# A quarter of batch 4's first product by Strassen's scheme, with four changes of order: the first chain, the w2 loads, S4, batch 5's attention

## The chip, the cores and the metric

The kernel runs on one core of one Trainium2 chip. The metric is the device time of one execution in microseconds. The core has a matrix engine (TensorE, PE in the profile), three engines for the rest (VectorE = DVE, ScalarE = ACT, GpSimd = POOL) and a queue engine (SyncE = SP) that here only issues DMA transfers. Each engine takes its instructions strictly in the order of the program and waits for the others by semaphores.

## What is computed

For each of 8 batches: linear attention with a cosine feature map over 8 heads (576 positions, head size 64), then a mixer: a low-rank product over the positions (U 576x32, V 32x576) with a residual, and a two-layer product over the 512 channels with 2048 hidden units.

```python
r = np.maximum(x, 0.0)                       # phi, for q and k
phi = np.concatenate([r * cos_w, r * sin_w], axis=-1)
kv = einsum('bhsf,bhsd->bhfd', k_p, v);  z = k_p.sum(axis=2)
x = einsum('bhsf,bhfd->bhsd', q_p, kv) / (einsum('bhsf,bhf->bhs', q_p, z) + 1e-6)
# heads side by side: x is [8, 576, 512]
u = x + (x.transpose(0, 2, 1) @ U @ V).transpose(0, 2, 1)
out = u + np.maximum(u @ w_ch1, 0.0) @ w_ch2
```

The large products are u @ w_ch1 (the first product) and the one with w_ch2 (the second).

## The kernel before

The 576 positions of a batch are 512 that are worked on as four chunks c of 128, and a tail of 64; the tails of two batches (a pair) are put together to one chunk of 128. All matmul operands are bf16, sums are float32 in PSUM (eight banks, which the code names by tags: "g" with three buffers, "T", "X" of two banks, "oA", "oB" or "O").

**The line of units.** After batch 0's attention everything is one hand-laid list of units of TensorE work (`slots`), most of them 0.9 us long. For each pair: the first product of the even batch (16 units of one hidden block j each), its second product, the first product of the odd batch, four units of the pair's tail, the second product of the odd batch, and for the first two pairs four more for the tail's second product. `starts[b]` is the slot at which batch b's first product begins. A second list (`todo`, by slot) holds what is issued behind each unit: the attention of the next batch, the feature maps, the DMA transposes and the loads. So the order on every engine follows from the slot numbers that `attention_plan` (L1097) gives.

**First product.** A plain unit is `g1_main` (L676): four matmuls of 512 columns into a "g" bank, then one ScalarE pass with the ReLU. `MIXED` (L789) names batches in which quarters m = 0 and 2 of the 16 hidden blocks go by Strassen's scheme instead: `g1_part` (L602) makes seven products of four matmuls of 256 columns each, and the eight units of HALF (L1015) interleave them with the four plain blocks of the next quarter. Parts 1, 6, 5, 3 add up in one bank (al_ps, tag T) that ScalarE copies out between them (pw), parts 2, 7, 4 in others (be_ps); VectorE adds and rectifies. They read differences of blocks of w1 (sa, made once, L571) and of u transposed (tb, `uT_form`, L590, four VectorE operations in the four slots ahead of `starts[b]`). Before, batches 3 and 5 are mixed in both quarters, batch 7 wholly, the others plain.

**Second product.** From batch 1 on it goes by Strassen's scheme: `w_part(b, n)` (L843) for n = 0 to 13 is half of one of seven steps, eight matmuls of 256 columns. I call n a half step. Step s is half steps 2s and 2s + 1. Steps 1, 2 and 3 open a bank each, steps 0 and 4 share one, step 5 adds into the bank of step 2, and step 6 into that of step 3, after VectorE has read it. Steps 1, 2, 3 and 5 read sums of hidden blocks (`hid_form`, L814): S1, S2 = S1 - hid, S3, S4 = hid - S2, each made in two halves on VectorE; the first halves beside the first product (L1035), the second halves by the table in L867. At half step 3 VectorE makes w_sum, then one block of the output on VectorE and two on GpSimd (L886 to L891).

**Attention of the next batch.** `kv_pair`, five `x_unit`s (matmuls, then denominator, reciprocal and product on VectorE), `A_unit` (U), `u_va` (V), `u_add` on VectorE, then `utr_dma`: the transposes of u (uT) as DMA transposes from SP's queue. The plan places them at slots counted from G = `starts[b - 1]`. For an odd batch b the tail follows (`u_tail`, and uT_tl). The loads of batch b + 1 and the transposes of q (q_tlT, q_pT) also go through SP's queue, in slot order.

**Batch 0** has no batch to hide behind. `first_chain` (L1232) runs its attention by hand: features, transposes of q, denominators (`den_mm`), kv in two groups of four heads, x, and uT on TensorE: `open_mm` puts x transposed into a bank, and `uTd_mm` adds the low-rank term (32 rows of the array each, d-th row group) and so closes it. `w1_load` and `w2_load` (L100, L106) are loads of 512 KB that GpSimd issues; a small copy into `mark` makes GpSimd wait for an event first (L1311, L1317, L1326). `gate` (L1340) does the same on SP: batch 2's loads wait for w2's second chunk.

Of the kernel before, what the change touches and what calls it, by code (L numbers as in the profile page):

```python
# [10 lines left out]
FP32 = mybir.dt.float32  # L11
BF16 = mybir.dt.bfloat16
# [5 lines left out]
def kernel(  # L18
# [93 lines left out]
    def cast(eng, o, i):  # L112
        if eng is nc.scalar:
            nc.scalar.activation(out=o, in_=i, func=AF.Copy, bias=0.0, scale=1.0)  # L114
        else:
            eng.tensor_copy(out=o, in_=i)  # L116
# [216 lines left out]
    def kv_unit(b, hg, tag, bufs, eng=None):  # L333
        if b not in kv_sb:
            kv_sb[b] = pool.tile([P, H, E], BF16, tag="kv", bufs=2, name="kv")
        n = D if b == 0 else E
        acc = bank([P, 4, n], FP32, tag, bufs, "kv_ps")
        for i in range(4):
            h = hg * 4 + i
            for c in range(5):  # L340
                nc.tensor.matmul(
                    out=acc[:, i, :],
                    lhsT=k_p[b][:, c, h, :] if c < 4 else k_tl[:, h, :],
                    rhs=v0[:, h, c, :] if b == 0 else vx_of(b, c, h),
                    start=(c == 0),
                    stop=(c == 4),
                )
        cast(eng or V_, kv_sb[b][:, hg * 4 : hg * 4 + 4, 0:n], acc)

    def kv_pair(b, tag, bufs):  # L350
        kv_sb[b] = pool.tile([P, H, E], BF16, tag="kv", bufs=2, name="kv")
# [200 lines left out]
    def uTd_evac(b, d, eng):  # L552
        cast(eng, uT[b][:, d, :, :], uT_ps[b, d])
# [232 lines left out]
                in_=o_s[i * TS : i * TS + TS, :],  # L786
            )

    MIXED = {3: (0, 2), 5: (0, 2)}  # L789
    HD = DM // 2  # L790
    KB = NJ // 2
    w2_h = w2_bf.rearrange("p (k i) n -> p k i n", i=2)
# [50 lines left out]
    def w_part(b, n):  # L843
# [16 lines left out]
        for k_ in range(half * 4, half * 4 + 4):  # L860
            for g in range(2):
# [2 lines left out]
                    start=(opens and k_ == 0 and g == 0),  # L864
                    stop=(k_ == KB - 1 and g == 1), skip_group_check=not opens,
                )
        for f in ({0: (4,), 2: (3,)} if b == B - 1 else {0: (1, 2), 2: (3,), 4: (4,)}).get(n, ()):  # L867
            hid_form(b, f, 1)
        if half == 0:
            return  # L870
# [219 lines left out]

    ODDX = (5, 8, 11, 13, 15)
    QORD = (4, 0, 1, 2, 3)

    def feature(b, f, c, i, eng):
        f(b, c, (eng, None) if i == 0 else (None, eng))

    def attention_plan(b):  # L1097
# [3 lines left out]
        def put(at, f, *a):  # L1101
            plan.append((at, lambda: f(b, *a)))
# [17 lines left out]
        else:  # L1120
# [16 lines left out]
            kv_at = X0  # L1137
            if late:
                kv_at, x_at = G + 3, [G + i for i in (5, 8, 13, 16, 18)]
            elif b - 1 in MIXED:  # L1140
                kv_at, x_at = G + 1, [G + i for i in ODDX]
            a_at = x_at[4] + (3 if b in (4, 6) else 2)
            u_at = a_at + 1
            a_bank = T1 if b == 3 else OB
# [6 lines left out]
            put(x_at[n], x_unit, c, *((O1, X1)[n % 2] if b < 4 else X1))  # L1151
        put(a_at, A_unit, *a_bank, A_)
        put(u_at, u_va, (0, *X1), (2, *O1) if b < 4 else (2, OA, OB))
        d0 = 2 if odd and b - 1 in MIXED else 0
        put(u_at, u_add, d0)
        put(u_at + 2, u_add, 2 - d0)
        put(u_at + 2, utr_dma, d0, d0 + 2)
        put(u_at + 4, utr_dma, 2 - d0, 4 - d0)
        if odd:
            put(*((u_at + 1, u_tail, *T1) if b < 4 else (u_at + 3 + d0, u_tail, *X1S)))  # L1160
            put(u_at + 4 + d0, utr_dma, 4, 5)
        if b < B - 1:
            for at_, t in zip(at_load, loads(b + 1)):
                plan.append((at_, t))
# [50 lines left out]
    def open_mm(b, d, t, cs):  # L1215
        for c in cs:
            nc.tensor.matmul(
                out=t[:, c, :], lhsT=x_bf[b][:, c, d * P : d * P + P], rhs=ident,
                start=(c == 0), stop=False,
            )  # L1220
# [11 lines left out]
    def first_chain(b, xz, z, v_ps):  # L1232
# [6 lines left out]

        d = xz[:, 1, 0:480].rearrange("p (c h n) -> p c h n", h=H, n=12)  # L1240
        rec = pool.tile([P, 5, H], FP32, tag="rec5", bufs=1, name="rec5")
        for h in (0, 2):
            cast(V_, v0[:, h : h + 2], vst[:, h : h + 2])
        cast(V_, z_sb, z[:, :, 0])
        qtr_evac(b, 2, V_, t_q[2])
        cast(V_, v0[:, 4:H], vst[:, 4:H])
        qtr_evac(b, 4, A_, t_q[4])
        kv_unit(b, 0, *G3, A_)
        cast(A_, V_bf, v_ps.rearrange("r (c p) -> r c p", c=4))
        den_mm(b, d, (0, 1, 3, 2, 4))  # L1250
        recip(rec, d[:, :, :, 0])
        x0 = [xh_mm(b, c, 0, *G3) for c in ORD[0:2]]
        kv_unit(b, 1, *T1, A_)
# [10 lines left out]
        cast(A_, A_of(b)[0:TS, :], a_ps[0:TS, :])  # L1264
        for i, (tag, bufs) in enumerate((OA, OB, T1)):
            uT_ps[b, i] = bank([P, 4, P], FP32, tag, bufs, "uT_ps")
        open_mm(b, 0, uT_ps[b, 0], range(4))
        x1.append(xh_mm(b, ORD[4], 4, *G3))
        for n in range(2, 5):
            xh_norm(b, ORD[n], 4, rec, x1[n])  # L1270
        uTd_mm(b, 0)
        uTd_evac(b, 0, A_)
        open_mm(b, 1, uT_ps[b, 1], range(4))
        uTd_mm(b, 1)
        uTd_evac(b, 1, A_)
# [17 lines left out]
    for c in TL:  # L1293
        q_prep(0, c, FEATS[c])
        qtr_mm(0, c, 0, H, t_q[c])
        keep_warm(1, "X", 1)
    for c, eng in zip(TL[0:2], (V_, A_)):
        qtr_evac(0, c, eng, t_q[c])
    xz = ps.tile([P, 2, 512], FP32, tag="X", bufs=1, name="xz")
    z = xz[:, 0, 0:384].rearrange("p (h n) -> p h n", n=48)  # L1300
# [22 lines left out]
    for h0 in (0, 4):  # L1323
        load_odd(vst, v, 1, h0, h0 + 4)
        load_even(vst, v, 1, h0, h0 + 4)
    G_.tensor_copy(out=mark, in_=kst[0:TS, 3, 4, 0:1])  # L1326
    for n in range(4):
        w2_load(n)
    g1_open(0, (0, 0), (0, 1))
    uTd_close(0, 2, V_)  # L1330
    uTd_close(0, 3, A_)
    g1_open(0, (0, 2), (1, 0), (1, 1), (1, 2))
    q_prep(1, 4, (V_, A_))
    q_prep(1, 0, (V_, V_))


    def at(j, *thunks):
        beside.setdefault(j, []).extend(thunks)

    def gate(src):  # L1340
        nc.sync.dma_start(out=mark2, in_=src)
# [102 lines left out]
```

## Time and profile before

| | us |
|---|---|
| median of three runs (292.41 to 292.49) | 292.44 |
| the profiled execution | 292.46 |
| its span | 290.7 |

| engine | busy us | share of the span | instructions |
|---|---|---|---|
| TensorE | 285.7 | 98% | 3062 |
| VectorE | 224.5 | 77% | 447 |
| ScalarE | 162.2 | 56% | 282 |
| GpSimd | 67.5 | 23% | 104 |

The granted clock of TensorE is 1.00 in every stretch but the last (0.99). A row of the timeline has the start, the length, the engine, the line of the kernel, the operation, what is written and read, the shape and the count; in square brackets stands the idle time before it, and who ended it. Matmuls overlap: a row's length contains the way through the array, so costs are taken from start to start, or from the chain of waits, whose pieces do not overlap. A group row has a count, then the busy time, then the mean length in ns, then the idle time ahead of it.

### The profile page before, as it was taken

Reading aid. Unit: us, or ns where it says so; the run is one execution under the profiler, and the core shown is the slowest. Engines: PE = TensorE matmul, PEld = TensorE weight load, DVE = VectorE, ACT = ScalarE, POOL = GpSimd, SP = SyncE. Lnnn points to the kernel's source line nnn. Section 1 sums busy time; section 2 is a strip of 40 time slices with the busy share of each in tenths; the row PEclk is TensorE's granted clock in tenths of the full one; section 3 lists DMA queues with packets and bytes.
Section 4 is the critical chain, followed back from the end, with each engine's and each line's share of the span. In section 5 each row is a group of like instructions: output and inputs, shape, how many; then the busy total and the mean of one; then the engine's idle time right before and its main releaser. Section 6 shows DMA issues by size and latency. Waiting matters only on the chain.

```text
span 290.7 us, 7417 instructions
## 1 busy us (share of the span) xinstructions
PE 285.7 (98%) x3062; PEld 206.0 (71%) x3062; DVE 224.5 (77%) x447; ACT 162.2 (56%) x282; POOL 67.5 (23%) x104
## 2 busy tenths in 40 slices
PE   8999999999999999999999999999999999999995
PEld 6876455545987546876986646876888548999884
DVE  4879748887898778948896377848899687769974
ACT  2965651576593456966693456966791562067100
POOL 8340500050052303640042500441031102100210
PEclk9999999999999999999999999999999999999999
DMA  6999999999939999799838995999186304120023
GB/s 200 337 283 253 261 186 264 297 245 221 287 86 153 231 357 194 216 278 265 237 58 181 229 281 100 249 249 291 18 145 77 148 12 81 49 99 0 2 87 132
DMA packets 85447, 53.32 MB, mean 183 GB/s; under 512 B 53990, under 2 KB 83078, under 8 KB 85414
## 3 DMA queue, kind: packets, MB, share of 16 engines
q1 hardware_dynamic: 78998, 41.62, 60.5%
q0 software_dynamic: 6272, 11.17, 15.8%
q8 instruction: 24, 0.39, 0.6%
q14 instruction: 9, 0.07, 0.1%
q10 hardware_dynamic: 144, 0.07, 0.1%
HBM read 36.86 MB, written 9.44 MB: 159 GB/s over the span
## 4 chain that ended last, share of the span: by engine, by line
PE 96%; DVE 2%; issue 1%; DVEq 0%
PE g_ps L684 29%; PE w_ps L862 28%; PE gt_ps L715 5%; PE o_ps L755 5%; PE al_ps L635 5%; PE be_ps L635 4%; PE w_ps L202 3%; PE x_ps L431 3%; PE kv_ps L356 2%; PE ot_ps L775 2%; PE ot_ps L963 2%; PE a_ps L457 1%; PE va_ps L487 1%; DVE u_bf L498 1%; PE t_ps L374 1%; PE t_ps L386 1%
## 5 line engine op out<-in xcount | busy, mean ns | idle before, releaser
L684 PE MATMUL g_ps<-uT,w_bf 128*128 128x512 bf16 x378 | 91.2, 379 | 0.0
L691 ACT ACTIVATE hid<-g_ps 128x512 bf16<-128x512 f32 x96 | 57.0, 597 | 44.6 <-PE g_ps L684 37.6
L684 PEld LDWEIGHTS <-w_bf 128*128 128x128 bf16 x378 | 34.3, 98 | 33.5
L874 POOL TENSOR_TENSOR o_sb<-w_sum,u_bf 128x512 f32<-128x512 f32 x14 | 22.1, 1595 | 117.5 <-DVE w_sum L874 117.5
L862 PEld LDWEIGHTS <-hid 128*128 128x128 bf16 x448 | 43.6, 98 | 5.6
L862 PEld LDWEIGHTS <-S 128*128 128x128 bf16 x336 | 32.3, 98 | 4.9 <-issue 0.5
L862 PE MATMUL w_ps<-T,hid 128*128 128x256 bf16 x224 | 26.9, 273 | 0.0
L862 PE MATMUL w_ps<-w_bf,hid 128*128 128x256 bf16 x224 | 26.9, 273 | 0.0
L862 PE MATMUL w_ps<-T,S 128*128 128x256 bf16 x224 | 26.3, 273 | 0.0
L652 DVE TENSOR_TENSOR hid<-pw,be_ps 128x512 bf16<-128x512 f32 x24 | 16.4, 685 | 11.9 <-ACT pw L114 7.6
L114 ACT ACTIVATE pw<-al_ps 128x512 f32<-128x512 f32 x24 | 14.2, 597 | 18.2 <-PE al_ps L635 17.4
L874 DVE TENSOR_TENSOR o_sb<-o_sb,w_ps 128x512 f32<-128x512 f32 x28 | 19.1, 682 | 4.9 <-PE w_ps L862 4.3
L498 DVE TENSOR_TENSOR u_bf<-x_bf,va_ps 128x1024 bf16<-128x1024 bf16 (+1 forms) x20 | 19.5, 1001 | 4.0 <-PE va_ps L487 3.9
L441 DVE TENSOR_TENSOR x_bf<-x_ps,rec 128x512 bf16<-128x512 f32 x28 | 19.3, 691 | 1.0
L305 ACT ACTIVATE k_p<-kst,sinw 128x512 bf16<-128x512 f32 x26 | 17.7, 712 | 0.0
L729 POOL DMA_DIRECT2D out_dram<-o_sb x12 | 7.6, 632 | 41.2 <-DVE o_sb L763 20.9
L116 POOL CAST v_ext<-vst 128x512 bf16<-128x512 f32 x24 | 15.6, 694 | 6.1 <-issue 3.7
L715 PE MATMUL gt_ps<-uT_tl,w_bf 128*128 128x128 bf16 x256 | 16.4, 219 | 0.0
L755 PE MATMUL o_ps<-w_bf,hid 128*128 128x512 bf16 x64 | 15.6, 379 | 0.0
L830 DVE TENSOR_TENSOR S<-hid,S 128x1024 bf16<-128x1024 bf16 x14 | 15.4, 1097 | 0.1
L715 PEld LDWEIGHTS <-w_bf 128*128 128x128 bf16 x256 | 15.0, 98 | 0.4
L305 ACT ACTIVATE q_p<-qst,cosw 128x512 bf16<-128x512 f32 x21 | 14.4, 712 | 0.0
(188 smaller groups left out, 472.7 us busy)
## 6 DMA issues: line engine op xcount, KB each, us to landing
qst<-in_q_dram SPq DMA_DIRECT2D x14, 512.0 KB, 6.3
kst<-in_k_dram SPq DMA_DIRECT2D x14, 512.0 KB, 8.2
vst<-in_v_dram SPq DMA_DIRECT2D x12, 512.0 KB, 7.9
out_dram<-o_sb POOLq DMA_DIRECT2D x12, 512.0 KB, 5.2
w_bf<-in_moe_w_ch_dram POOLq DMA_DIRECT2D x8, 512.0 KB, 10.2
out_dram<-o_sb SPq DMA_DIRECT2D x4, 512.0 KB, 3.0
qst<-in_q_dram SPq DMA_DIRECT2D x2, 640.0 KB, 5.8
kst<-in_k_dram SPq DMA_DIRECT2D x2, 640.0 KB, 13.8
```

Of the source, the lines that this page charges most:

```text
L116: eng.tensor_copy(out=o, in_=i)
L305: nc.scalar.activation(out=o, in_=i, func=AF.Relu, bias=0.0, scale=w)
L441: nc.vector.tensor_tensor(out=x_of(b, c, rows).rearrange("p (g i d) -> p g i d", g=2, d=D), in0=view[:, :, :, 0:D], in1=rec[rows].unsqueez ...
L498: nc.vector.tensor_tensor(out=u_bf[b][:, d0 : d0 + n], in0=x_bf[b].rearrange("p c (d n) -> p d c n", n=P)[:, d0 : d0 + n], in1=t.rearrange ...
L635: nc.tensor.matmul(out=res[:, k_, :], lhsT=lhs[:, d, k_, :], rhs=rhs[:, d, :], start=(opens and k_ == 0 and d == 0), stop=(k_ == 1 and d = ...
L652: V_.tensor_tensor(out=o, in0=x, in1=res, op=ALU.add)
L684: nc.tensor.matmul(out=g_ps.rearrange("p (c t) -> p c t", c=4), lhsT=w1_bf[:, d, j * P : j * P + P], rhs=uT[b][:, d, :, :], start=(d == 0) ...
L691: nc.scalar.activation(out=hid[b][:, j, :], in_=g_ps, func=AF.Relu, bias=0.0, scale=1.0)
L715: nc.tensor.matmul(out=g_ps[:, jj, :], lhsT=w1_bf[:, d, j * P : j * P + P], rhs=uT_tl[pr][:, d, :], start=(d == 0), stop=(d == 3),)
L755: nc.tensor.matmul(out=o, lhsT=hid[0][:, j, cc * P : cc * P + P], rhs=w2_bf[:, j, :], start=(j == 0), stop=(j == NJ - 1),)
L862: nc.tensor.matmul(out=res[:, g, :], lhsT=lhs[:, k_, g * P : g * P + P], rhs=rhs[:, k_, :], start=(opens and k_ == 0 and g == 0), stop=(k_ ...
L874: eng.tensor_tensor(out=o, in0=x, in1=y, op=ALU.add)
```

## The change

1. Batch 4's quarter m = 0 becomes mixed; the list of batches with both quarters mixed gets a name (`FULL`). Two rules that asked "is batch b - 1 mixed" now ask for `FULL`. What follows for batch 4 is that its first eight units are those of HALF, that `uT_form` runs ahead of it, and that the first halves of its S forms go to units 9, 11, 17 and 18 of its own (8 to 11 before); the last two lie in its second product.
2. For batch 5, whose attention runs beside batch 4, kv moves from slot G - 2 to G + 1, the x units from G + 0, 2, 4, 6, 8 to G + 5, 8, 11, 13, 15, `A_unit` to G + 17, `u_va` to G + 18; uT's transposes to G + 20 and G + 22, and the tail one slot later than the formula had it. Batch 4's second product begins at G + 16. On SP's queue batch 7's loads of v now stand ahead of batch 5's uT, and batch 6's q_tlT between the two of them.
3. In the second product, the second half of S4 is made at half step 1 instead of 4 (batches 1 to 6).
4. In batch 0's chain the third copy of q transposed comes ahead of k's features on VectorE; kv of the first four heads and the denominators alternate; uT is opened for d = 0 and 1, then closed for both, then copied out; d = 2 and 3 are closed ahead of the six openings of the first product, which stood around them.
5. GpSimd waits for batch 1's last q transposed, in slot 6, instead of for batch 1's k, before it issues the four w2 loads.

```diff
-    MIXED = {3: (0, 2), 5: (0, 2)}
+    MIXED = {3: (0, 2), 4: (0,), 5: (0, 2)}
+    FULL = [b for b, ms in MIXED.items() if 2 in ms]
...
-        for f in ({0: (4,), 2: (3,)} if b == B - 1 else {0: (1, 2), 2: (3,), 4: (4,)}).get(n, ()):
+        for f in ({0: (4,), 2: (3,)} if b == B - 1 else {0: (1, 2), 1: (4,), 2: (3,)}).get(n, ()):
             hid_form(b, f, 1)
...
+    X5 = (5, 8, 11, 13, 15)
...
+            elif b - 1 in FULL:
+                kv_at, x_at = G + 1, [G + i for i in ODDX]
             elif b - 1 in MIXED:
-                kv_at, x_at = G + 1, [G + i for i in ODDX]
+                kv_at, x_at = G + 1, [G + i for i in X5]
...
-        d0 = 2 if odd and b - 1 in MIXED else 0
+        d0 = 2 if odd and b - 1 in FULL else 0
...
         if odd:
-            put(*((u_at + 1, u_tail, *T1) if b < 4 else (u_at + 3 + d0, u_tail, *X1S)))
-            put(u_at + 4 + d0, utr_dma, 4, 5)
+            late_t = 1 if b - 1 in MIXED and b - 1 not in FULL else 0
+            put(*((u_at + 1, u_tail, *T1) if b < 4 else (u_at + 3 + d0 + late_t, u_tail, *X1S)))
+            put(u_at + 4 + d0 + late_t, utr_dma, 4, 5)
...
-        for h in (0, 2):
-            cast(V_, v0[:, h : h + 2], vst[:, h : h + 2])
+        cast(V_, v0[:, 0:2], vst[:, 0:2])
         cast(V_, z_sb, z[:, :, 0])
-        qtr_evac(b, 2, V_, t_q[2])
+        cast(V_, v0[:, 2:4], vst[:, 2:4])
         cast(V_, v0[:, 4:H], vst[:, 4:H])
         qtr_evac(b, 4, A_, t_q[4])
-        kv_unit(b, 0, *G3, A_)
+        kv_sb[b] = pool.tile([P, H, E], BF16, tag="kv", bufs=2, name="kv")
+        acc = bank([P, 4, D], FP32, *G3, "kv_ps")
+        kv0_mm(b, acc, (0, 1))
+        den_mm(b, d, (0, 1, 2))
+        kv0_mm(b, acc, (2, 3))
         cast(A_, V_bf, v_ps.rearrange("r (c p) -> r c p", c=4))
-        den_mm(b, d, (0, 1, 3, 2, 4))
+        cast(A_, kv_sb[b][:, 0:4, 0:D], acc)
+        den_mm(b, d, (3, 4))
...
-        open_mm(b, 0, uT_ps[b, 0], range(4))
+        for i in range(2):
+            open_mm(b, i, uT_ps[b, i], range(4))
         x1.append(xh_mm(b, ORD[4], 4, *G3))
...
-        uTd_mm(b, 0)
-        uTd_evac(b, 0, A_)
-        open_mm(b, 1, uT_ps[b, 1], range(4))
-        uTd_mm(b, 1)
-        uTd_evac(b, 1, A_)
+        for i in range(2):
+            uTd_mm(b, i)
+        for i in range(2):
+            uTd_evac(b, i, A_)
...
-    for c, eng in zip(TL[0:2], (V_, A_)):
+    for c, eng in zip(TL[0:3], (V_, A_, V_)):
         qtr_evac(0, c, eng, t_q[c])
...
-    G_.tensor_copy(out=mark, in_=kst[0:TS, 3, 4, 0:1])
-    for n in range(4):
-        w2_load(n)
-    g1_open(0, (0, 0), (0, 1))
-    uTd_close(0, 2, V_)
-    uTd_close(0, 3, A_)
-    g1_open(0, (0, 2), (1, 0), (1, 1), (1, 2))
+    for d in (2, 3):
+        uTd_mm(0, d)
+    uTd_evac(0, 2, V_)
+    uTd_evac(0, 3, A_)
+    g1_open(0, *((d, j) for d in range(2) for j in range(3)))
...
+    def w2_all():
+        G_.tensor_copy(out=mark[0:1], in_=q_pT[1][0:1, 3, 0, 0:1])
+        for n in range(4):
+            w2_load(n)
+
+    at(6, w2_all)
```

`kv0_mm` is new: the five matmuls over the chunks of `kv_unit` for the heads that it is given, without the copy.

More of the change, by code (lines that the diff above doesn't have):

```diff
@@ L348, in kv_unit, with kv0_mm @@
         cast(eng or V_, kv_sb[b][:, hg * 4 : hg * 4 + 4, 0:n], acc)
+    def kv0_mm(b, acc, hs):
+        for h in hs:
+            for c in range(5):
+                nc.tensor.matmul(
+                    out=acc[:, h, :], lhsT=k_p[b][:, c, h, :] if c < 4 else k_tl[:, h, :],
+                    rhs=v0[:, h, c, :], start=(c == 0), stop=(c == 4),
+                )
     def kv_pair(b, tag, bufs):
```

## The prediction

> **What bounds the kernel now.** I read the page first, then the chain of waits in order of time, then the timelines of TensorE, VectorE and GpSimd around each edit.
>
> ```profile
> span 290.7 us, 7417 instructions
> ...
> PE 96%; DVE 2%; issue 1%; DVEq 0%
> ```
>
> The span is 290.7 us, the profiled execution itself took 292.46 us, so 1.76 us lie around the span; the three plain runs have a median of 292.44 us, and I treat the two as one number. The second row is the chain that ended last: 96% of it is TensorE. So the time is the sum of what TensorE executes plus the few places where it stands still. Anything on another engine counts only where TensorE waits for it. Following TensorE's starts through the timeline, I find waits in batch 0's chain (16 to 19 us) and two more:
>
> ```profile
> 151.65 1.91 PE L862 MATMUL w_ps<-w_bf,hid 128*128 128x256 bf16 x16
> 153.73 1.91 PE L862 MATMUL w_ps<-w_bf,S 128*128 128x256 bf16 x16 [0.17 <-DVE o_sb L874]
> ...
> 217.63 1.91 PE L862 MATMUL w_ps<-w_bf,hid 128*128 128x256 bf16 x16
> 219.56 1.91 PE L862 MATMUL w_ps<-w_bf,S 128*128 128x256 bf16 x16
> ```
>
> These are starts, lengths and counts. Sixteen such matmuls take 1.75 us from start to start (16 x 0.109, below); here 153.73 - 151.65 = 2.08 and 219.56 - 217.63 = 1.93. So TensorE loses 0.33 us in batch 3's second product and 0.18 us in batch 5's, both ahead of step 5 (half step 10), which adds into the PSUM bank that VectorE must first have read in step 2.
>
> **The quarter of batch 4.** It replaces 16 plain matmuls of 512 columns by 7 parts of 4 matmuls of 256 columns.
>
> ```profile
> 101.16 2.59 PE g_ps L684 x12
> ...
> 258.00 1.31 PE al_ps L635 x12
> ```
>
> From the chain: 2.59 / 12 = 0.216 us and 1.31 / 12 = 0.109 us. 16 x 0.216 = 3.45 us go, 28 x 0.109 = 3.06 us come: **-0.40 us**. Beside TensorE, ScalarE keeps four passes, and VectorE gets three additions (0.69 each) with three rectifications (0.3) and four differences of uT (0.4): 4.6 us.
>
> ```profile
> 160.00:180.00 20.00, 20.00 (x207) 10.95 (x204) 12.34 (x26) 10.93 (x19) 3.92 (x7) 1.00 0.91 213
> ```
>
> In this view of stretches the columns are TensorE, its weight loads, VectorE, ScalarE, GpSimd, the granted clock, DMA. VectorE works 12.34 of the 20 us around batch 4's first product, so 7.7 us hide the 4.6, and ScalarE is no fuller; batches 3 and 5 run the same eight units today with no TensorE wait in them. Cost: nothing. Without that cover a late addition would hold a PSUM bank, and TensorE for as long.
>
> The Trainium skill speaks against this edit (TensorE: Matmul & The Clock Gate, Back-to-back issue gap): in a sustained stream a matmul of 512 columns costs 131 ns and one of 128 columns 81 ns, so narrow ones are dear. By an estimate between those figures, about 98 ns for 256 columns, the quarter would lose 0.6 us instead. The trace disagrees with both figures (216 and 109 ns); the sum goes by the rows.
>
> **Batch 5's attention moves later.** With batch 4 mixed, kv and the x units of batch 5 slide to units 1, 5, 8, 11, 13, 15, and its A, va and u_tail groups leave batch 4's first product for its second. TensorE does the same work, with the same number of changes between 32-row and 128-row matmuls. But VectorE now has three additions to u (and u_tail), and two half forms (S4, S3), in the second product, behind which the step 2 read waits. I work out that queue, counted from the first matmul W of the second product.
>
> ```profile
> 171.27 0.16 DVE L421 TENSOR_SCALAR rec<-x_ps 128x8 f32<-128x8 f32 x1
> ...
> 172.30 0.68 DVE L830 TENSOR_TENSOR S<-S,hid 128x1024 bf16<-128x1024 bf16 x1
> ...
> 179.21 0.69 DVE L830 TENSOR_TENSOR S<-hid 128x1024 bf16<-128x1024 bf16 x1 [0.90 <-ACT hid L691]
> 179.94 0.69 DVE L830 TENSOR_TENSOR S<-S,hid 128x1024 bf16<-128x1024 bf16 x1
> 180.55 0.47 DVE L307 TENSOR_SCALAR q_tl<-qst,sinw 64x512 bf16<-64x512 f32 x1
> 180.94 0.47 DVE L307 TENSOR_SCALAR q_p<-qst,sinw 128x512 bf16<-128x512 f32 x1
> ```
>
> The last x unit ends at W, its three VectorE instructions take 172.30 - 171.27 = 1.03: 1.07. S1 and S2 0.73 + 0.61: 2.41. q feature 0.39: 2.80. Two halves of S4, 0.61 each: 4.02. Feature 0.39, two halves of S3: 5.63. Then u (1024 wide, two of 0.6): 6.83. Feature: 7.22. w_sum and o_sb, 0.7 + 0.6: 8.5. Two more u additions (1.19, from 151.81 to 153.00 below): 9.7. The step 2 read 0.67: **W + 10.4**.
>
> ```profile
> 110.39 0.34 PE va_ps L510 x8
> ...
> 145.63 0.39 PE a_ps L457 x20
> 146.03 0.98 PE w_ps L862 x8
> ```
>
> TensorE arrives there after ten half steps of 8 x 0.109 = 0.87 us, with a_ps (0.39), va_ps (as the 0.34 of L510), u_tail (0.34), and three times the 0.11 by which the half step behind such a group is longer (0.98): 8.73 + 1.07 + 0.33 = 10.1. So a new wait of about **+0.2 us**; I bound it by 0 (VectorE ahead by one feature) and 0.9 (one more 0.69 row in front of it).
>
> The uT transposes move with it. The second one can be issued at W + 9.7, behind batch 6's q_tlT on SP's queue, and is needed by the third matmul of batch 5's first plain group: 10.1 + 0.2 + 4 x 0.87 + 0.44 + 0.43 = W + 14.7, and by the differences (tb) just after. Leave is thus 5.0 us.
>
> ```profile
> DMA to landing us min/median/max: 3.2/3.4/6.0
> ```
>
> This is the tile view of uT. At the median it lands 1.6 us early: 0; at the maximum it costs 1.0. Behind it on SP stand uT_tl, batch 6's q_pT and batch 7's q and k loads, some 7 us later than now; by the lengths in the DMA list their landings still come about 2 us ahead of the first readers (batch 6's second x unit, batch 7's features): 0, and beyond that leave one for one. Batch 7's v loads go ahead of uT on SP, but are issued long before it, when GpSimd's casts of v are done.
>
> **S4's second half two steps sooner.** Now it stands behind w_sum and o_sb on VectorE, and so runs beside GpSimd's additions:
>
> ```profile
> 149.68 3.23 POOL L874 TENSOR_TENSOR o_sb<-w_sum,u_bf 128x512 f32<-128x512 f32 x2 [18.34 <-DVE w_sum L874]
> ...
> 150.24 1.65 DVE L830 TENSOR_TENSOR S<-hid,S 128x1024 bf16<-128x1024 bf16 x1
> 151.81 1.27 DVE L498 TENSOR_TENSOR u_bf<-x_bf,va_ps 128x512 bf16<-128x512 bf16 x2
> 153.00 1.47 DVE L874 TENSOR_TENSOR o_sb<-o_sb,w_ps 128x512 f32<-128x512 f32 x2
> ```
>
> The same form takes 0.69 us where GpSimd rests (179.94) and 1.65 here, until GpSimd's first addition is over; the u additions and o_sb behind it, also beside GpSimd, keep their 0.6 to 0.7. Moved ahead of w_sum it takes 0.69, and the step 2 read comes 0.96 us sooner. Both stalls (0.33, 0.18) are smaller than that: **-0.51 us**. In the other batches TensorE does not wait there, so nothing follows. My W + 10.4 has the short form in it.
>
> The Trainium skill (SBUF — State Buffer, SBUF: two separate sides) has a rule for the long row: a VectorE operation with two SBUF inputs and a GpSimd operation that reads SBUF take a shared port in turn, and the later one stands until the other instruction ends. The trace agrees (150.24 to the end of a 1.6 us addition, then 0.6); without it, if the 1.65 were S4's own, the sum would lose its -0.51.
>
> **Batch 0's chain.** Two closes of uT in different row groups come together, as the second pair does now:
>
> ```profile
> 19.47 0.38 PE L557 MATMUL uT_ps<-V_bf,A_sb 32*128 32x512 bf16 x1
> ...
> 20.43 0.40 PE L457 MATMUL a_ps<-x_bf,U_bf 128*32 128x128 bf16 x8
> ...
> 21.06 0.39 PE L1217 MATMUL u<-ident,x_bf 128*128 128x128 bf16 x4
> 21.28 0.59 PE L701 MATMUL g_ps<-uT,w_bf 128*128 128x512 bf16 x2
> 21.81 0.39 PE L557 MATMUL uT_ps<-V_bf,A_sb 32*128 32x512 bf16 x1
> 21.81 0.38 PE L557 MATMUL u<-V_bf,A_sb 32*128 32x512 bf16 x1
> ```
>
> Close, open, close takes 20.43 - 19.47 = 0.96 now. The pair at 21.81 starts at once, so two closes cost what one does (0.32), and an open without a change of rows costs 0.22 (21.06 to 21.28): 0.54, a gain of 0.42. Against it:
>
> ```profile
> 10.52 0.61 PE L386 MATMUL t_ps<-ident,q_p 128*128 128x128 bf16 x8
> ...
> 14.60 0.28 PE L341 MATMUL kv_ps<-v,k_p 128*128 128x64 bf16 x4
> ...
> 11.48 1.28 DVE L307 TENSOR_SCALAR k_p<-kst,cosw 128x512 bf16<-128x512 f32 x3 [0.71 <-DMA kst<-in_k_dram]
> ...
> 13.87 0.89 DVE L116 CAST v<-vst 128x640 bf16<-128x640 f32 x2
> ...
> 18.82 1.40 DVE L1203 TENSOR_TENSOR x_bf<-xh_ps,rec 128x256 bf16<-128x256 f32 x4
> ```
>
> The third q_pT copy (0.6) now starts when its transposes end (11.13), inside the 0.71 us that VectorE waits for k, but overruns it by 0.29. The first v0 cast ends at 13.87 + 0.45 + 0.29 = 14.6, where kv would start: about 0.1 late. The second a_ps group then starts sooner than the last x (20.22 + 0.1) is there: another 0.1. So **-0.2 us**, between 0 and -0.42. Splitting kv and den in pairs leaves TensorE's count as it is, and den's end, for which the reciprocals wait.
>
> **w2 sooner.** The loads wait for batch 1's last q_pT copy instead of k.
>
> ```profile
> 29.32 0.69 DVE L116 COPY q_pT<-t_ps 128x1024 bf16<-128x1024 bf16 x1 [0.45 <-PE t_ps L374]
> ...
> 32.34 2.97 POOL L108 DMA_DIRECT2D w_bf<-in_moe_w_ch_dram  x4 [0.27 <-issue]
> ...
> 38.86 1.03 PE L755 MATMUL o_ps<-w_bf,hid 128*128 128x512 bf16 x4
> ```
>
> First issue at about 30.4 for 32.34.
>
> ```profile
> w_bf<-in_moe_w_ch_dram POOLq DMA_DIRECT2D x1, 512.0 KB, 6.3
> ```
>
> By this DMA row of the first chunk it lands at 38.7 now, just ahead of its reader at 38.86, which comes 0.2 us sooner: without this edit the two would meet. It shares the DMA with v of batch 1, whose readers stand 2 us ahead of kv. I take 0, between -0.1 and +0.3.
>
> **Sum.** -0.40 + 0.2 - 0.51 - 0.2 + 0 = -0.91 us: 292.46 - 0.91 = **291.5 us**. The ends: -0.40 - 0.51 - 0.42 - 0.1 = -1.43 (291.0); -0.40 + 0.9 - 0.51 + 0.3 = +0.3 (292.8) if all go badly at once, which I hold for rare.
>
> **Rivals.** *Batch 5's uT is late* (slower). Its second transpose queues behind a transpose of the next row, 6.1 us to landing in the median:
>
> ```profile
> q_tlT<-q_tl SPq DMA_TRANSPOSE x6, 6.1
> ```
>
> From a landing of 5.0 us on TensorE stands, and from 6.5 on the whole is more than 0.58 slower. At 7.4 the price is 2.4: 293.9 us. For it: SP issues the two within 1.5 us. Against: the rows' 3.4. Chance 0.10. *The wait at half step 10 takes the gain* of batch 4: 0.9 in place of 0.2: 292.2 us, no change. For it: VectorE is full there; against: the queue above, row by row. Chance 0.14. *The stalls do not go*, because S4's 1.65 is its own: 292.0 us; against it the 0.69 rows. Chance 0.08. *Narrow matmuls are dearer in a mixed quarter*: break-even is 0.123 us; at 0.13 the sum is -0.3, 292.2 us. Batches 3 and 5 show 0.109; chance 0.01. That is where the skill's rule above would lead. The forecast keeps 0.67.
>
> **How the numbers follow.** 0.2% (0.58 us) is about what can be told from no change. The forecast lies beyond it: faster 0.67. The last three rivals make same 0.14 + 0.08 + 0.01 = 0.23, the first one slower 0.10. The range reaches from 291.0 up to 292.4, past the rivals at 292.0 and 292.2, and leaves out the late transpose.
>
> **What would show it.** No TensorE gap above 0.1 us ahead of half step 10 in batches 3 and 5, S4's second half at 0.69 in all batches, a gap of 0.0 to 0.3 there in batch 4; 28 parts of 0.109 in batch 4's first quarter; both closes of uT starting together near 19.8; uT's second transpose landing over a microsecond ahead of batch 5. Wrong: a TensorE wait for uT or tb at batch 5's start, a wait at o_ps for w2, or a wait in batch 4's step 5 over 0.5 us.

## The result and the profile after

The changed kernel takes 291.90 us in the median of 20 runs (291.62 to 293.34), the kernel before 292.52 us in 20 runs beside them: a ratio of 0.9978 with a 95% interval of 0.9968 to 0.9988, or 0.62 us less. Forecast were 291.5, so the direction held, and a third of the gain did not come.

| | before | after, first profile | after, second profile |
|---|---|---|---|
| profiled execution, us | 292.46 | 292.69 | 292.01 |
| its span, us | 290.69 | 290.66 | 290.07 |

The first profile of the changed kernel fell on one of its longer executions, and would mislead if it were read alone. The second one (run e5, below) is 0.62 us shorter in its span than before, which is just the difference of the medians, so I divide the time by it. All of the difference lies in four stretches; the rest (from the first o_ps to batch 3's second product, and from batch 6's second product to the end) agrees to 0.02 us in these three profiles.

| stretch, from TensorE start to TensorE start | before | after, first | after, second |
|---|---|---|---|
| span's start to the first A group (xz from x_bf) | 18.63 | 19.37 | 18.67 |
| first A group to batch 1's first q transposes | 5.24 | 4.94 | 4.94 |
| from there to the first o_ps (w2's first reader) | 14.99 | 14.99 | 15.10 |
| second product of batch 3 to second product of batch 6 | 97.04 | 96.57 | 96.58 |

So +0.04 - 0.30 + 0.11 - 0.46 = -0.61, the 0.62 of the spans but for rounding. The second and the fourth row come back in every profile of this order of instructions (to 0.03 and 0.01 us). The first and the third do not: they contain waits for loads, and with the changed chain the first A group starts anywhere between 18.54 and 19.37 us. Their +0.04 and +0.11 belong to these two executions, and can't be put down to the change. First the fourth row, in which parts 1, 2 and 3 of the change meet. This is the view of stretches, TensorE's start to start, of the kernel before and then of the second profile after; the columns are length, TensorE, weight loads, VectorE, ScalarE, GpSimd, clock, busy share of the DMA engines, GB/s.

```profile
143.72:178.38 34.66, 34.49 (x355) 22.15 (x353) 25.20 (x45) 20.09 (x34) 8.41 (x11) 1.00 0.73 166
178.38:209.70 31.32, 31.32 (x346) 25.64 (x344) 23.84 (x49) 23.41 (x40) 7.42 (x9) 1.00 0.81 198
209.70:240.76 31.06, 31.04 (x339) 20.57 (x337) 26.83 (x54) 18.62 (x33) 4.49 (x4) 1.00 0.51 99
```

```profile
143.58:176.12 32.54, 32.38 (x321) 22.84 (x322) 23.85 (x46) 19.80 (x34) 7.97 (x11) 1.00 0.90 229
176.12:209.27 33.15, 32.73 (x390) 26.12 (x390) 27.70 (x58) 23.53 (x41) 6.96 (x9) 1.00 0.69 161
209.27:240.16 30.89, 30.73 (x336) 20.64 (x337) 26.20 (x54) 18.64 (x33) 4.04 (x4) 1.00 0.49 99
```

The first two stretches must be read together, since batch 5's attention moves from the one into the other: 65.98 before, 65.69 after; the third gives 0.17 more. What is to be read here is the lengths. The busy times beside them don't show a wait as it is: of a wait between two starts only the part behind the end of the pipeline counts as idle, and a matmul whose record is missing (the counts differ by a few) looks idle too. Waits are read from the starts in the timeline; this is TensorE's after, first profile, at batch 4's half step 10:

```profile
185.09 1.91 PE L871 MATMUL w_ps<-w_bf,hid 128*128 128x256 bf16 x16
187.25 1.91 PE L871 MATMUL w_ps<-w_bf,S 128*128 128x256 bf16 x16 [0.26 <-DVE o_sb L883]
```

2.16 from start to start, where sixteen such matmuls take 1.75: a wait of 0.41. The bracket shows only 0.26 of it, because the first row's length of 1.91 reaches to 187.00; it names VectorE's read of step 2. VectorE's timeline there:

```profile
177.35 0.69 DVE L449 TENSOR_TENSOR x_bf<-x_ps,rec 128x512 bf16<-128x512 f32 x1
177.96 0.68 DVE L839 TENSOR_TENSOR S<-hid 128x1024 bf16<-128x1024 bf16 x1
...
179.68 1.28 DVE L839 TENSOR_TENSOR S<-hid,S 128x1024 bf16<-128x1024 bf16 x2
180.88 0.47 DVE L307 TENSOR_SCALAR q_p<-qst,sinw 128x512 bf16<-128x512 f32 x1
181.28 1.28 DVE L839 TENSOR_TENSOR hid<-hid 128x1024 bf16<-128x1024 bf16 x2
182.48 1.21 DVE L506 TENSOR_TENSOR u_bf<-x_bf,va_ps 128x1024 bf16<-128x1024 bf16 x1
...
185.32 1.28 DVE L506 TENSOR_TENSOR u_bf<-x_bf,va_ps 128x512 bf16<-128x512 bf16 x2
186.52 0.68 DVE L883 TENSOR_TENSOR o_sb<-o_sb,w_ps 128x512 f32<-128x512 f32 x1
```

From the last x unit's product on (177.35) one instruction stands behind the other without a gap, and the read that TensorE needs ends at 187.20, 10.49 us behind the second product's first matmul W (176.71). In batches 3 and 5 the same place is clean:

```profile
152.10 1.91 PE L871 MATMUL w_ps<-w_bf,hid 128*128 128x256 bf16 x16
153.84 1.91 PE L871 MATMUL w_ps<-w_bf,S 128*128 128x256 bf16 x16
...
217.80 1.91 PE L871 MATMUL w_ps<-w_bf,hid 128*128 128x256 bf16 x16
219.54 1.91 PE L871 MATMUL w_ps<-w_bf,S 128*128 128x256 bf16 x16
```

1.74 in both, for 2.08 and 1.93 before. The second row of the table is batch 0's chain, again TensorE after, first profile:

```profile
19.79 0.62 PE L1230 MATMUL uT_ps<-ident,x_bf 128*128 128x128 bf16 x8
20.25 0.29 PE L1207 MATMUL xh_ps<-kv,q_pT 128*128 128x64 bf16 x4
20.47 0.39 PE L565 MATMUL uT_ps<-V_bf,A_sb 32*128 32x512 bf16 x2
20.79 0.50 PE L465 MATMUL a_ps<-x_bf,U_bf 128*32 128x128 bf16 x8
21.10 0.23 PE L465 MATMUL a_ps<-x_tl,U_bf 128*32 128x128 bf16 x2
21.27 0.40 PE L1230 MATMUL uT_ps<-ident,x_bf 128*128 128x128 bf16 x4
```

Both closes start together (x2 at 20.47) and take 0.32 before the second A group follows. From the first opening to that group it is 1.00 us (19.79 to 20.79), where it was 1.41: before, the first opening started at 19.02 and the group at 20.43.

```profile
19.02 0.40 PE L1217 MATMUL uT_ps<-ident,x_bf 128*128 128x128 bf16 x4
```

The A group itself takes 0.48 to the next opening (20.79 to 21.27) where it took 0.39 (20.43 to 20.82): VectorE's last x ends at 20.99, inside it.

### The profile page after: what moved, and what is told of

Read it like the earlier page. It is cut to its first block, busy times and chain, and to the rows that moved or that the text cites. A ratio compares the mean times of both kernels' runs of the same rounds, so it can differ in the third digit from the quotient of the medians.

```text
span 290.7 us, 7429 instructions
## 1 busy us (share of the span) xinstructions
PE 282.3 (97%) x3049; PEld 205.9 (71%) x3074; DVE 222.9 (77%) x457; ACT 161.8 (56%) x282; POOL 65.6 (23%) x104
## 4 chain that ended last, share of the span: by engine, by line
PE 91%; DVE 4%; DMA 2%; issue 1%; ACT 0%; DVEq 0%; ACTq 0%
PE g_ps L692 27%; PE w_ps L871 27%; PE al_ps L643 6%; PE gt_ps L723 5%; PE o_ps L763 5%; PE be_ps L643 4%; PE x_ps L439 3%; PE kv_ps L364 2%; DMA qst<-in_q_dram 2%; PE ot_ps L783 2%; PE ot_ps L972 2%; PE a_ps L465 1%; PE va_ps L495 1%; DVE S L839 1%; PE t_ps L394 1%
## 5 line engine op out<-in xcount | busy, mean ns | idle before, releaser
L692 PE MATMUL g_ps<-uT,w_bf 128*128 128x512 bf16 x345 | 85.8, 379 | 0.7
L699 ACT ACTIVATE hid<-g_ps 128x512 bf16<-128x512 f32 x92 | 54.6, 597 | 42.6 <-PE g_ps L692 32.5
L692 PEld LDWEIGHTS <-w_bf 128*128 128x128 bf16 x362 | 33.1, 98 | 31.5
L883 POOL TENSOR_TENSOR o_sb<-w_sum,u_bf 128x512 f32<-128x512 f32 x14 | 19.5, 1408 | 122.6 <-DVE w_sum L883 122.6
L114 ACT ACTIVATE pw<-al_ps 128x512 f32<-128x512 f32 x27 | 16.0, 596 | 26.1 <-PE al_ps L643 15.1
L660 DVE TENSOR_TENSOR hid<-pw,be_ps 128x512 bf16<-128x512 f32 x27 | 18.5, 686 | 15.0 <-ACT pw L114 7.9
L116 POOL CAST v_ext<-vst 128x512 bf16<-128x512 f32 x24 | 16.7, 739 | 5.8 <-issue 3.7
L643 PEld LDWEIGHTS <-sa 128*128 128x128 bf16 x144 | 13.4, 98 | 2.9 <-issue 0.2
L723 PEld LDWEIGHTS <-w_bf 128*128 128x128 bf16 x256 | 15.0, 98 | 0.4
L305 ACT ACTIVATE q_p<-qst,sinw 128x512 bf16<-128x512 f32 x18 | 12.5, 713 | 3.9 <-DMA qst<-in_q_dram 3.8
```

Source lines behind the costliest of these rows:

```text
L305: nc.scalar.activation(out=o, in_=i, func=AF.Relu, bias=0.0, scale=w)
L643: nc.tensor.matmul(out=res[:, k_, :], lhsT=lhs[:, d, k_, :], rhs=rhs[:, d, :], start=(opens and k_ == 0 and d == 0), stop=(k_ == 1 and d = ...
L660: V_.tensor_tensor(out=o, in0=x, in1=res, op=ALU.add)
L692: nc.tensor.matmul(out=g_ps.rearrange("p (c t) -> p c t", c=4), lhsT=w1_bf[:, d, j * P : j * P + P], rhs=uT[b][:, d, :, :], start=(d == 0) ...
L699: nc.scalar.activation(out=hid[b][:, j, :], in_=g_ps, func=AF.Relu, bias=0.0, scale=1.0)
L723: nc.tensor.matmul(out=g_ps[:, jj, :], lhsT=w1_bf[:, d, j * P : j * P + P], rhs=uT_tl[pr][:, d, :], start=(d == 0), stop=(d == 3),)
```

## The experiments

Beside every group of experiments (e1 to e4, e5 to e8, e9 to e11, e12) the kernel before ran on the same chip, so ratios can be compared, medians only within a group. The stretches of a profile, on the other hand, repeat from run to run to a few hundredths of a microsecond wherever no DMA is waited for; most of the verdicts rest on them. A number in brackets behind a ratio is its 95% interval.

**e1: S4's second half alone**, on the kernel before.

```diff
-        for f in ({0: (4,), 2: (3,)} if b == B - 1 else {0: (1, 2), 2: (3,), 4: (4,)}).get(n, ()):
+        for f in ({0: (4,), 2: (3,)} if b == B - 1 else {0: (1, 2), 1: (4,), 2: (3,)}).get(n, ()):
```

> The kernel before with one edit: S4's second half at half step 1 instead of 4. Theory (S4 stood beside GpSimd and made the step 2 read late): all second halves of S4 take 0.69 us, the TensorE gaps of 0.33 and 0.18 us ahead of half step 10 in batches 3 and 5 are gone, the time falls by 0.5 us to about 292.0. Rival (S4's 1.65 us is its own length, or TensorE waits for something else there): the gaps stay and the time is that of before, 292.5.

292.16 us, ratio 0.9963 (0.9939 to 0.9986). From batch 3's second product to batch 6's the profile has 96.52 us for 97.04: -0.52. The timeline of e1 in batch 3, VectorE and then TensorE:

```profile
146.62 0.69 DVE L830 TENSOR_TENSOR S<-hid,S 128x1024 bf16<-128x1024 bf16 x1
```

```profile
152.06 1.91 PE L862 MATMUL w_ps<-w_bf,hid 128*128 128x256 bf16 x16
153.81 1.91 PE L862 MATMUL w_ps<-w_bf,S 128*128 128x256 bf16 x16
```

The form takes 0.69 (1.65 before), and the stall is gone (1.75 from start to start). GpSimd's pair of additions, which the form no longer meets, is shorter too: 2.77 for 3.23 us.

```profile
150.53 2.77 POOL L874 TENSOR_TENSOR o_sb<-w_sum,u_bf 128x512 f32<-128x512 f32 x2 [18.79 <-DVE w_sum L874]
```

So the long row was not S4's own. The rule of the Trainium skill that the prediction cited (SBUF — State Buffer, SBUF: two separate sides), that the two engines hold a shared port in turn, agrees with both numbers.

**e2: batch 0's chain alone**, on the kernel before (part 4 of the change). Some lines of its edit:

```diff
+        for i in range(2):
+            open_mm(b, i, uT_ps[b, i], range(4))
...
+        for i in range(2):
+            uTd_mm(b, i)
...
+    for c, eng in zip(TL[0:3], (V_, A_, V_)):
```

> The kernel before with batch 0's chain of the change alone (third q_pT copy ahead of k, kv and denominators in turn, uT closed in pairs); w2 waits for k as before. Theory (pairs save 0.42, the longer VectorE queue ahead of kv and of the second A group gives 0.2 back): 0.2 us faster, 292.3; from the first transpose of q to the first plain unit 13.6 us instead of 13.8. Rival (in the profile after, kv begins 0.32 later counted from the first transposes): nothing is left, 292.5. A wait of the o_ps units for w2 would make it slower.

292.41 us, ratio 0.9995 (0.9968 to 1.0022): no difference to be told. In its profile the first A group starts at 18.70 (before 18.63), batch 1's transposes at 23.62 (23.87): 4.92 us between them for 5.24, so the part behind the first A group gives its 0.3 here too. What stands ahead of that group can't be compared: VectorE waits 0.91 us for batch 0's v in this execution. Another 0.08 goes at o_ps, which waits for w2 (15.07 us behind the transposes in place of 14.99), although w2 is issued as before.

**e3: all but the quarter of batch 4**, on the kernel after.

```diff
-    MIXED = {3: (0, 2), 4: (0,), 5: (0, 2)}
+    MIXED = {3: (0, 2), 5: (0, 2)}
```

> The changed kernel with batch 4 plain again (and so batch 5's attention at its old slots); the other edits stay. Theory (in the profile after, the quarter's 0.40 us go into a wait of 0.42 ahead of half step 10 of batch 4): the same time as the changed kernel, 291.9, with no gap in batch 4's second product. Rival (the quarter earns its 0.40 and the wait is an accident of one execution): 0.2 to 0.4 slower than the changed kernel, 292.2.

291.86 us, ratio 0.9965 (0.9942 to 0.9989). The stretches of batches 3 to 5 are 34.33 + 31.31 + 30.88 = 96.52 us, 0.05 less than with the quarter (96.57). The quarter of batch 4, the part that gives the change its name, is worth nothing as it stands.

**e4: two S forms of batch 4 sooner**, on the kernel after. The first halves of S2, S4 and S3 go to units 10, 12 and 14 in place of 11, 17 and 18, that is, back beside the first product.

```diff
-            n = 12 + 2 * i if b == 1 else (9, 11, 17, 18)[i] if b in MIXED else 8 + i
+            n = 12 + 2 * i if b == 1 else (9, 10, 12, 14)[i] if b == 4 else (9, 11, 17, 18)[i] if b in MIXED else 8 + i
```

> The changed kernel with the first halves of batch 4's S forms at units 9, 10, 12 and 14 of its first product, so that S4 and S3 (0.6 us each) no longer stand in VectorE's queue of the second product. Theory (that queue makes the wait): VectorE's step 2 read comes 1.2 us sooner, the 0.42 us gap ahead of half step 10 is gone, 0.4 faster than the changed kernel: 291.5. Rival (the wait is for another event, or the two forms now hold up an x unit): 291.9 or more.

291.60 us, ratio 0.9961 (0.9937 to 0.9984). The view of stretches, second product of batch 4 to that of batch 5:

```profile
176.66:209.40 32.74, 32.74 (x394) 26.14 (x391) 26.57 (x56) 23.50 (x41) 6.95 (x9) 1.00 0.70 165
```

This is the stretch of 33.15 us (e5), now 0.41 shorter. At half step 10 TensorE goes on after 1.75 us (184.65 to 186.40 in e11, the same kernel), and batches 3 to 5 take 96.16 us: 0.41 less than after, 0.36 less than without the quarter (e3). So the quarter's own saving is there, 0.36 for the 0.40 of the sum, and the wait had eaten it.

**e5: the kernel after once more.** 

> The changed kernel once more. Theory: its executions come in two kinds, set by when batch 0's loads land; in the usual kind batch 1's first q transposes start at 23.6 us of the span (24.3 in the profile at hand), with a span of 289.9 to 290.0 us, and the median is 291.9. Rival: the 24.3 is the chain's own time, then the next profile shows 24.3 again and a span of 290.7. In both, batch 3's and 5's second products stand still nowhere for over 0.1 us and batch 4's waits 0.4 us ahead of half step 10.

292.03 us, ratio 0.9975 (0.9954 to 0.9996). Batch 1's transposes start at 23.61 in it, with the span of 290.07 that the first section uses. Nothing in the program differs from the first profile. The loads landed otherwise: q at 8.0 us in this one and at 8.8 in the first.

**e6: the sooner w2 alone**, on the kernel before (part 5 of the change).

```diff
-    G_.tensor_copy(out=mark, in_=kst[0:TS, 3, 4, 0:1])
-    for n in range(4):
-        w2_load(n)
...
+    def w2_all():
+        G_.tensor_copy(out=mark[0:1], in_=q_pT[1][0:1, 3, 0, 0:1])
+        for n in range(4):
+            w2_load(n)
+
+    at(6, w2_all)
```

> The kernel before with only the w2 loads sooner. Theory: 0, within 0.1 us of the kernel before; o_ps starts 14.99 us after batch 1's first q transposes, as before. Rival: the sooner loads hold up batch 1's v and with it kv: 0.1 to 0.3 us slower between those two starts.

292.85 us beside 292.82, ratio 0.9993 (0.9972 to 1.0013): no difference in the time. But theory and rival both missed what its profile shows: the stretch to o_ps is 15.75 us, 0.76 more than before, and not by v and kv, but by w2 itself. TensorE's timeline, and the DMA list for the issue of the first chunk (at 30.83; KB and us to landing):

```profile
39.84 1.02 PE L755 MATMUL o_ps<-w_bf,hid 128*128 128x512 bf16 x4 [0.59 <-DMA w_bf<-in_moe_w_ch_dram]
```

```profile
w_bf<-in_moe_w_ch_dram POOLq DMA_DIRECT2D x1, 512.0 KB, 9.0
```

Issued 1.5 us sooner than before (32.34), the chunk lands 1.2 us later (39.8 for 38.6): it takes 9.0 us in place of 6.3. The loads of this execution were slow from earlier on (w1's third chunk landed at 31.1 for 28.6), so this one row doesn't show that the sooner issue does harm, only that it doesn't help.

**e7 and e8: parts of the chain undone**, on e4. In e7 only the closes in pairs are left of part 4; in e8 only the third copy of q transposed is put back behind v's second cast, and the denominators that read it change places with those of the next chunk. Of e8's edit:

```diff
-    for c, eng in zip(TL[0:3], (V_, A_, V_)):
+    for c, eng in zip(TL[0:2], (V_, A_)):
...
         cast(V_, v0[:, 2:4], vst[:, 2:4])
+        qtr_evac(b, 2, V_, t_q[2])
```

> The changed kernel with the S forms of batch 4 made sooner (as in the run with 291.60 us), and of the new chain of batch 0 only the closes in pairs: the third copy of q transposed and the order of kv and denominators are the old ones again. Theory (the copy ahead of k costs 0.3 us when q's load lands late, and nothing when it lands early; the closes are worth 0.42): from the first q transposes to the first A group 9.44 us when they start at 9.2 or later, 10.5 when they start at 8.4; from there to batch 1's transposes 4.9; median 291.5 or less. Rival (alternating kv and denominators is what gains): 0.2 us slower than the run with 291.60, so 291.8.

> As the run before this one, but with kv and denominators alternating; only the third copy of q transposed is back behind z and the second cast of v on VectorE. Theory (the copy ahead of k is what costs): first q transposes to first kv 5.4 us when they start at 9.2 or later, where the changed kernel has 5.74; to the first A group 9.4 to 9.5; median 291.4 to 291.6. Rival (the copy in its old place holds up v's last cast and so the reciprocals): first A group 0.3 us later than in the kernel with the copy in front.

291.85 us, ratio 0.9975 (0.9950 to 1.0000), and 291.98 us, ratio 0.9968 (0.9949 to 0.9987). The times do not tell them from e4. The theory of both expectations was that the copy costs the time by which it holds up k's features. With the copy back, the first A group starts 10.20 (e7) and 10.15 us (e8) behind the first q transposes; with the copy in front 9.77 (e5), so the theory misses, and the rival of e8 (0.3 later with the copy back) seems to fit. But with the copy in front other executions have 9.55 (e12) to 10.28 (e2, e3), so this comparison decides nothing. What differs between e5 and e8 is in VectorE's timeline, first of e5, then of e8:

```profile
10.56 1.28 DVE L116 COPY q_pT<-t_ps 128x1024 bf16<-128x1024 bf16 x2
11.76 1.27 DVE L307 TENSOR_SCALAR k_p<-kst,cosw 128x512 bf16<-128x512 f32 x3
```

```profile
9.88 0.68 DVE L116 COPY q_pT<-t_ps 128x1024 bf16<-128x1024 bf16 x1
11.88 1.28 DVE L307 TENSOR_SCALAR k_p<-kst,cosw 128x512 bf16<-128x512 f32 x3 [1.32 <-DMA kst<-in_k_dram]
```

In e8 k was not there before 11.88, and the 1.32 us of waiting would have held the copy of 0.6 twice. In the first profile after, q was late and VectorE did not wait for k. By these rows, what the copy costs or saves hangs on when k lands, and that differs between executions of one program. Counted from VectorE's start on k to the first A group, and leaving out executions with another wait of over half a microsecond in between (e1, e2, e3, e11: 7.42 to 7.68), the old order takes 7.01 to 7.15 us (before, e6, e7) and the new one 6.91 to 6.97 (both profiles after, e4, e9, e10, e12); e8 has 7.05. That is 0.04 to 0.24 less, but the copy has left this stretch for the time ahead of it, so whether the new order gains anything on balance is not shown.

Both executions also show a wait that neither expectation has: o_ps starts 15.58 (e7) and 15.45 us (e8) behind batch 1's transposes, 0.59 and 0.46 later than 14.99, and waits for w2. This is e7:

```profile
39.53 1.02 PE L763 MATMUL o_ps<-w_bf,hid 128*128 128x512 bf16 x4 [0.42 <-DMA w_bf<-in_moe_w_ch_dram]
```

**e9, e10, e11: when w2 is issued**, side by side on e4. e9 has the old gate for all four chunks, e10 the new one for the first chunk and the old one for the other three, e11 is e4 itself.

```diff
         G_.tensor_copy(out=mark[0:1], in_=q_pT[1][0:1, 3, 0, 0:1])
-        for n in range(4):
+        w2_load(0)
+        G_.tensor_copy(out=mark, in_=kst[0:TS, 3, 4, 0:1])
+        for n in range(1, 4):
             w2_load(n)
```

> The kernel of the 291.60 us run (S forms of batch 4 sooner), but with the four w2 loads issued behind batch 1's k again, as before the change. Theory (the first w2 chunk lands when the queue of loads ahead of it is through, between 38.6 and 39.8 us of the span, whether it is issued at 30.5 or at 32): it is issued at about 32 and lands at 38.6 to 39.3, batch 1's last v lands 1 to 3 us sooner than with the sooner w2, and the first matmul that reads w2 waits 0 to 0.4 us for it, as it did in the profiles with the sooner one; median 291.5 to 291.9, no difference. Rival (w2 sooner is what lets the first chain's gain through): the wait is 0.5 us or more, median 292.2.

> The same kernel, with only w2's first chunk issued sooner (behind batch 1's last q transposed); the other three wait for batch 1's k again. Theory (the chunk shares the DMA engines with the other three and with v): it lands 0.5 us or more sooner than with all four sooner, by 38.5, and the first matmul that reads w2 waits for nothing; between batch 1's first q transposes and that matmul 14.99 us; median 291.3 to 291.6. Rival (the chunks of one queue go one after the other, so the other three take nothing from the first): it lands as before, 7.6 to 8.9 us behind its issue, and the median is that of all four sooner.

> The kernel of the 291.60 us run once more, beside the two above, on the same chip. Theory: TensorE stands nowhere ahead of half step 10 in batches 3, 4 and 5, and the sum of batches 3 to 5 (from the first second product of batch 3 to that of batch 6) is 96.16 us as there, 0.41 less than in the changed kernel; median 291.5 to 291.9, by how w2 lands.

291.87 us (ratio 0.9964, 0.9946 to 0.9981), 291.49 us (0.9966, 0.9948 to 0.9983) and 291.68 us (0.9959, 0.9945 to 0.9973): no difference that the intervals allow. In all three o_ps starts 14.99 us behind batch 1's transposes. The issue of the loads on GpSimd's queue in e9, and the first chunk in the DMA lists of e9 and of e10 (there issued at 30.18):

```profile
32.34 2.97 POOL L108 DMA_DIRECT2D w_bf<-in_moe_w_ch_dram  x4 [0.27 <-issue]
```

```profile
w_bf<-in_moe_w_ch_dram POOLq DMA_DIRECT2D x1, 512.0 KB, 6.1
```

```profile
w_bf<-in_moe_w_ch_dram POOLq DMA_DIRECT2D x1, 512.0 KB, 8.2
```

32.34 + 6.1 and 30.18 + 8.2 give 38.4 both: two microseconds of head start bring nothing. Over all profiles the first chunk lands between 38.0 and 39.8 us with the sooner gate (ten profiles) and between 38.4 and 39.2 with the old one (before, e1, e2, e9). The other three chunks are not what holds it up either (with all four sooner e11 has 30.61 + 7.7 = 38.3), so the theory of e10 fell. That the backlog of loads issued before them (w1's last chunks, batch 1's k and v) sets the landing would fit these rows, but is not shown: a run that thins out that backlog was not made. With the sooner gate v mostly lands later: batch 1's last v at 35.5 to 36.1 us with the old gate and at 36.1 to 40.7 with the sooner one (35.5 in e9, 36.4 in e11, 40.7 in e6).

**e12: one form out instead of two**, on e10. Of batch 4's forms S4's first half goes back to unit 17 and S2's to 11; S3's stays at 14.

```diff
-            n = 12 + 2 * i if b == 1 else (9, 10, 12, 14)[i] if b == 4 else (9, 11, 17, 18)[i] if b in MIXED else 8 + i
+            n = 12 + 2 * i if b == 1 else (9, 11, 17, 14)[i] if b == 4 else (9, 11, 17, 18)[i] if b in MIXED else 8 + i
```

> The kernel with only w2's first chunk sooner, but of the two S forms of batch 4 that had been taken out of its second product only S3's first half stays out (unit 14); S4's first half is back beside the second product's first half step. Theory (VectorE is one queue without gaps there, 0.42 us too long): 0.6 us less in it takes the whole wait away, TensorE stands nowhere ahead of half step 10 of batch 4, and from the first second product of batch 3 to that of batch 6 are 96.16 us, as with both forms out. Rival (each of the two forms holds TensorE for itself, by its own readers): half of the wait, 0.2 us, is left, 96.37 us.

291.56 us, ratio 0.9941 (0.9904 to 0.9978; the runs of the kernel before spread from 292.38 to 296.07 beside it). TensorE's timeline at half step 10, then VectorE's read of step 2:

```profile
184.31 1.91 PE L871 MATMUL w_ps<-w_bf,hid 128*128 128x256 bf16 x16
186.06 1.91 PE L871 MATMUL w_ps<-w_bf,S 128*128 128x256 bf16 x16
```

```profile
185.14 0.68 DVE L883 TENSOR_TENSOR o_sb<-o_sb,w_ps 128x512 f32<-128x512 f32 x1
```

1.75 from start to start: one row of 0.6 less on VectorE takes the whole wait of 0.42 away, and batches 3 to 5 take 96.15 us, as with two rows. S4's row is back in the queue, and the read ends at 185.82, 9.89 us behind W (175.93) where it was 10.49, and 0.24 ahead of TensorE. So the rival, that each form holds TensorE for itself, is out; it is one queue, and only its length counts.

e4 and e10 to e12 are thus the better version: the changed kernel with one or two S forms of batch 4 beside the first product. The 0.41 us rests on the profiles. The times don't show it: all runs with the forms moved (e4, e7 to e12, with other edits in some) have ratios of 0.9941 to 0.9975, the changed kernel 0.9978 and 0.9975, and the intervals overlap.

## Why the prediction was right, and where it was not

- **S4's second half.** Predicted -0.51, measured -0.52 (e1), with the mechanism that was named: the form at 0.67 to 0.69 ahead of w_sum, the read of step 2 sooner, the gaps ahead of half step 10 gone. By the times this part alone (0.9963) can't be told from the whole change (0.9978).
- **The quarter of batch 4.** Predicted -0.40, measured -0.36 once nothing waits (e4 against e3). The narrow matmuls cost what the rows said; neither the loss of 0.6 by the figures of the Trainium skill (TensorE: Matmul & The Clock Gate, Back-to-back issue gap) nor the rival at 0.13 us came true.
- **The new wait.** Here the sum failed: predicted +0.2, measured +0.42. The place, the order of the queue and the term on the other side were right: TensorE would have arrived at 185.09 + 1.75 = 186.84, W + 10.13 (predicted 10.1). VectorE's end came at W + 10.49 (predicted 10.4), and 0.05 more pass until the first matmul starts. With their second digits the prediction's own terms are 10.38 and 10.13, a wait of 0.25. The term that was too short is the first one of VectorE's queue: the last x unit was to end at W + 1.07, and S1 starts behind it at 177.96, W + 1.25. The ten terms behind it took 9.24 for 9.31. So 0.25 + 0.18 - 0.07 + 0.05 = 0.41, and the whole gain of the quarter was gone. A difference of two sums of 10 us was given to a tenth, where its size decided about the edit. The rival "the wait takes the gain of batch 4" came true in its effect, at half its price.
- **Batch 5's uT.** The slower rival fell. SP's queue after, first profile, and the DMA list for the third of its rows:

```profile
183.72 1.24 SPq L535 DMA_TRANSPOSE uT<-u_bf  x1
185.07 1.26 SPq L413 DMA_TRANSPOSE q_tlT<-q_tl  x1
186.63 1.45 SPq L535 DMA_TRANSPOSE uT<-u_bf  x1
```

```profile
uT<-u_bf SPq DMA_TRANSPOSE x1, 3.4
```

  186.63 + 3.4 is 190.0, 0.7 us ahead of batch 5's first matmul at 190.74 and 1.6 ahead of the one that by the prediction's count needs it (190.74 + 0.44 + 0.43 = 191.6), as the sum had it. TensorE shows no wait for uT there. The slow transpose of the next row in front of it (q_tlT) did not slow it.
- **Batch 0's chain.** The pair gave 0.41 of its 0.42 (1.41 to 1.00 us), the second A group's wait took its 0.1, -0.30 behind the first A group in all; this came back in every run with the closes in pairs. The 0.1 that was set down for the third copy as a constant could not be measured: what the copy does depends on k's landing (e7, e8). In the second profile the chain gives -0.26, near the -0.2 of the sum, but the +0.04 in it hangs on the loads of two executions.
- **w2 sooner.** Predicted 0, between -0.1 and +0.3; the medians of e6 and e9 say 0. The profiles add that o_ps waits for w2's first chunk in some executions, with the sooner gate (0.11 in e5, 0.46 in e8, 0.59 in e7, 0.76 in e6) and with the old one (0.08 in e2, 0.18 in e1). The prediction named such a wait as a sign of being wrong; it expected the sooner issue to prevent it, and the sooner issue does not.

By the second profile: batch 4 +0.05 for -0.2, S4 -0.52 for -0.51, the chain -0.26 for -0.2, w2 +0.11 for 0: -0.62 for -0.91. Of this, +0.05, -0.52 and -0.30 of the chain repeat from profile to profile; the rest is how the loads of these executions landed. That the forecast of the direction held rests on S4's form and the closes in pairs; the quarter did nothing for it.

## What to carry to other kernels

When an edit moves work into a stage where one engine's queue already ends near the point at which another needs it, the difference of the two arrivals is the price, and it is worth all the digits that the rows give; one row of 0.6 us too many there cost as much as the narrow matmuls saved. It is often enough to move a single row out, so look for one that has leave elsewhere before judging the edit. And a load that is issued sooner need not land sooner: here two microseconds of head start moved nothing, so compare landings, not issues.

## What the runs showed of the hardware that was not expected

One program's start differs between executions by over a microsecond: the first q transposes began between 8.4 and 9.6 us of the span, with q landing between 7.3 and 8.8 us. The two profiles of the changed kernel lie 0.6 us apart in their spans by this, while their later stretches agree to 0.02 us, but for o_ps's wait of 0.11 for w2.

In two profiles (e2, e11) TensorE stood still in the midst of batch 0's denominators for no reason that the profile shows; this row is from e11:

```profile
16.41 0.31 PE L1199 MATMUL xz<-z_sb,q_tlT 128*128 128x12 bf16 x6 [0.51 <-issue]
```

The reciprocals wait for these matmuls, and e11's first A group came 10.17 us behind the first q transposes, against 9.56 in e10, the same instructions up to there. In e2 the stop is hidden, as VectorE is still waiting for v. What ends the stop was not found.
